# Where the second-level factors of w_out are summed: from row blocks in SBUF in the first group instead of from DRAM later, and two more products on two levels

## The chip, the cores and the metric

The kernel runs on one core of one Trainium2 chip. The time is that of one execution on the device, in microseconds (us), as the median of several runs. Before the change it is 671.21 us (three runs, 670.92 to 671.93).

## The reference

```python
# attention: batch 4, 8 heads, 768 positions, head size 64, blocks of 64 positions
intra = einsum('bhic,bhjc->bhij', qb, kb) * Dmask      # Dmask[i, j] = lam**(i-j) for i >= j
out   = einsum('bhij,bhjd->bhid', intra, vb) + einsum('bhid,bhde->bhie', qb * lam_pow, kv_state)
kv_state = lam_block * kv_state + einsum('bhsd,bhse->bhde', kb * rev_pow, vb)
# then, with x = out as (3072 tokens, 512)
h = x @ w_in                       # w_in (512, 2048), float64 on arrival
g = h - tanh(h)
result = g @ w_out                 # w_out (2048, 512), float64 on arrival
```

Everything is computed in fp32. Almost all of the time is in the two large matrix products.

## The kernel before

**Groups.** The 3072 tokens are taken in six groups (g = 0 to 5) of 512: 128 positions of each of the four batch entries. In a group, `up` computes the hidden values from x and w_in, the tanh step follows, and `down` computes the result from the hidden values and w_out. The attention of the next group is worked in between, in pieces (`att_transpose`, `att_scores`, `att_out`, `att_state`, `att_sums`), first for batch entries 0 and 1, then for 2 and 3.

**Products by Strassen and Winograd.** Both factors of a product are split in 2 x 2 blocks. Seven block products, numbered 1 to 7, take the place of eight; they need sums of blocks: S1 to S4 on one side, T1 to T4 on the other. `FACT` names the two factors of each of the seven: B11, B21, B22, T4, T1, T2 and T3 for products 1, 2, 3, 4, 5, 6 and 7 of `down`. A product of `down` on one level is sixteen matmuls (32 records in the profile, as an fp32 matmul shows as two) of 128x128 against 128x256. On two levels the same product is split once more in the same way: seven small products of four matmuls, 28 matmuls (56 records) of 128x128 against 128x128. `down` (lines 645 to 676) does the first and `down_twice` (696 to 732) the second; `twice(g, n)` says which product goes which way. Before the change the second group (g = 1) does products 5 and 6 on two levels, groups 2 to 4 do 3, 5, 6, 4 and 7, and the last group does 5, 6, 4 and 7.

**The first group.** Its `up` is plain. Its `down` goes over eight pairs of row blocks of w_out (`kt` = 0 to 7): rows kt x 128 and those 1024 further down, each split in two column halves, give b11, b12, b21 and b22. `round_block` makes fp32 of a loaded float64 block: ScalarE writes a copy into the pair's buffer and two halves of an addend, VectorE shifts the copy and adds. `sums_out(kt)` subtracts on VectorE to make T1, T2, T3 and T4 of that pair. `down_first` issues the matmuls of the pair, two for each of the seven products, which add up in seven PSUM banks (`acc`) over all eight pairs. `sums_late(kt)` makes two sums of the hidden values, the first of which overwrites what product 1 of this pair reads and is read by product 6. For a pair TensorE takes products 1, 2, then 5, 4, 7, 6, 3. `first_results` adds the seven banks up. Pairs have three buffers in turn: two of the pool `wst` and one made of `ws_3` and `ws_2`, which are free until the second group.

**Factors in DRAM.** `factors` holds the first-level factors, `fine` the seven second-level factors of each of five products (3, 5, 6, 4, 7). Of these seven, three are quarters of the first-level factor (small products 1, 2 and 3, one column half of an even or odd pair's rows), and `sums_out` stores them straight from the pair. The other four are sums of quarters. Before the change these are made in groups 1 and 2: `load_quarters` reads the four quarters of a first-level factor back from `factors`, and `factors_twice` makes four subtractions on VectorE and stores each result to `fine`, one at a time between other work, at the steps that `turns` gives: products 5 and 6 in the second group, 4, 7 and 3 in the third.

**Pieces.** The second factors of `down` come from DRAM as pieces of 256 KB through a ring of seven buffers (`wb`). `stream` lists them in the order of use, and `piece` hands out one and sends the loads of the next, on the queue of POOL (GpSimd).

**What sets the order.** Each engine works its instructions in order. A scheduler of the language orders them when the program is built, by its own estimate of when each is ready; `tc.keep_in_program_order` (also through `tied`) pins an instruction behind the one written just before it for the same engine. A tile with a tag takes one of the tag's buffers (`bufs`) and waits until the tile that had it is done. SyncE (SP) issues the loads of q, k and v, pinned in program order. From the third group on, k and v are loaded whole for two or three batch entries (`load_natural`, tags `k` and `v`, three and four buffers), and q and k also in blocks for transposes on VectorE (`load_blocks`, sixteen DMAs a tile, tag `blk`). In SP's order for a group stand k and v of entries 0 to 2 (third group) and then the eight tiles of blocks, with k and v of entry 3 after them.

Of the kernel before, what the change touches and what calls it, by code (L numbers as in the profile page):

```python
# [24 lines left out]
def kernel(  # L25
# [32 lines left out]
    nc = tc.nc  # L58
# [122 lines left out]
    NX = 7  # L181
# [40 lines left out]
    def weights(n):  # L222

        while ready["done"] < min(n, len(blocks)):
# [5 lines left out]
            w = w1[n_][:, m] if kind == "in" else pair[n_][0][:, 2 * m:2 * m + 2]  # L230
# [6 lines left out]
    def pair_tiles(kt):  # L237

        if kt % 3 == 2:
            return tuple(ws[u].rearrange("p x k c -> p (x k) c")[:, 0:4] for u in (3, 2))  # L240
        wt = wst.tile([128, 8, 256], F32, name="wt", tag="w")
        return wt[:, 0:4], wt[:, 4:8]
# [8 lines left out]
    def sums_out(kt):  # L251
        bt, tt = pair[kt]
        b11, b12, b21, b22 = (bt[:, x] for x in range(4))
        t1, t2, t4, t3 = (tt[:, x] for x in range(4))
        nc.vector.tensor_tensor(t1, b12, b11, op=AL.subtract)
# [12 lines left out]

    def round_block(w, raw64, first):
# [13 lines left out]
        tied(first, nc.vector.tensor_scalar(out=wb, in0=wb, scalar1=3, scalar2=None, op0=AL.logical_shift_left))  # L283
        nc.vector.tensor_tensor(wi, wi, add, op=AL.add)  # L284
# [264 lines left out]
    def twice(g, n):  # L549
        return n in TWICE and not (g == NG - 1 and n == 3) and not (g == 1 and n in (4, 7, 3))  # L550
# [27 lines left out]
    MADE = (5, 6, 4, 7, 3)  # L578
    quarters = {}

    def quarter_source(t, i, j):
        return factors[XAT[FACT[MADE[t]][1]]].rearrange("p (u m) c -> p u m c", m=2)[:, :, i, ts(j, 128)]

    def load_quarters(t):

        for i in range(2):
            for j in range(2):
                if t > 1:
                    quarters[t, i, j] = piece(2, ("quarter", t), 2 * i + j).rearrange("p m (v c) -> p (m v) c", v=2)
                    continue  # L590
                if t == 0:
                    x = late["pool"].tile([128, NU, 128], F32, name="wq", tag="wb", bufs=RING)
                else:
                    x = opool.tile([128, NU, 128], F32, name="oq", tag="o")
                nc.gpsimd.dma_start(out=x, in_=quarter_source(t, i, j))
                quarters[t, i, j] = x

    def factors_twice(t):

        b11, b12, b21, b22 = (quarters.pop((t, i, j)) for i in range(2) for j in range(2))  # L600
        t1, t2, t4 = (late["pool"].tile([128, NU, 128], F32, name=f"wt{x}", tag="sums", bufs=4) for x in (1, 2, 4))
        for x, dst, a, b in ((5, t1, b12, b11), (6, t2, b22, t1), (7, b12, b22, b12), (4, t4, b21, t2)):
            tc.keep_in_program_order(nc.vector.tensor_tensor(dst, a, b, op=AL.subtract))
            nc.gpsimd.dma_start(out=fine[TWICE.index(MADE[t]), SUB.index(x)], in_=dst)
            yield

    def piece(g, n, x):

        i = stream.index((g, n, x))
        while sent["n"] < min(i + RING, len(stream)):  # L610
            g_, n_, x_ = stream[sent["n"]]
            t = late["pool"].tile([128, 2, 256], F32, name="wb", tag="wb", bufs=RING)
            if isinstance(n_, tuple) and n_[0] == "quarter":
                nc.gpsimd.dma_start(out=t.rearrange("p m (v c) -> p (m v) c", v=2),
                                    in_=quarter_source(n_[1], *divmod(x_, 2)))
# [160 lines left out]
    FIRST = {1: (11, 0, 0), 2: (21, 0, 2), 3: (21, 0, 3), 4: (22, 1, 2), 5: ("S1", 1, 0), 6: (11, 1, 1), 7: (12, 1, 3)}  # L776
# [18 lines left out]
    def sums_late(kt):  # L795
        u, m = divmod(kt, 2)
        g11, g21, s1 = (hidden(0, c)[:, u, m] for c in (11, 21, "S1"))
        nc.vector.tensor_tensor(g11, s1, g11, op=AL.subtract)
        nc.vector.tensor_tensor(g21, g21, g11, op=AL.subtract)
# [76 lines left out]
    for kt in range(KH):  # L876
# [15 lines left out]
    turns = {1: (0, ((0, 7), (1, 14))), 2: (7 * NU, ((2, 1), (3, 5), (4, 9)))}  # L892
    made, making = [], {}
    load_quarters(0)
    load_quarters(1)
    up(1, 0, 1)
    for g in range(1, NG):
        last = g == NG - 1
        p0, p1 = attention(g + 1) if not last else ([], [])
        for u in range(NU):  # L900
            for n in (2, 6, 5, 7, 1, 4, 3) if g < GI else (1, 7, 3) if u == 0 else (6, 5, 1, 7, 3) if u + 1 < NU else (
# [9 lines left out]
                if g in turns:  # L911
                    made.append(n)
                    step = len(made) - turns[g][0]
                    for t, first in turns[g][1]:
                        if step == first:
                            if t > 1:
                                load_quarters(t)
                            making[t] = factors_twice(t)
# [71 lines left out]
```

## Time and profile before

| | before |
|---|---|
| median of the runs | 671.21 us |
| the profiled execution: time, span | 669.39 us, 667.6 us |
| TensorE (PE) busy | 655.6 us, 98% |
| VectorE (DVE) busy | 466.4 us, 70% |
| ScalarE (ACT) busy | 213.7 us, 32% |
| GpSimd (POOL) busy | 210.8 us, 32% |
| DMA | 128.82 MB, mean 193 GB/s |
| granted clock of TensorE | 1.0 |

The stretches of the span that matter here (us from its start): the pairs of the first group's `down`, 98.6 to 147.1; the second group's `up`, 147.1 to 204; its `down`, 204 to 262; the third group's `up` after that, to about 308. In a profile line the first number of a timeline row is the start, the second how long the row lasts from its first instruction's start to its last one's end; "x32" counts merged instructions, and a bracket tells how long the engine was idle before and what ended that. "L446" is a line of the kernel. In rows of waits the numbers are us in total, times, and the longest. A matmul's end is modelled, so lengths of products are read from start to start. "PEq", "SPq" and "POOLq" are the engines' queues.

### The profile page before, as it was taken

How to read it: one execution, taken by the hardware profiler on the slowest of the kernel's cores; microseconds unless marked ns; L12 is line 12 of the kernel's file. 1: busy time of each engine (PE TensorE's matmuls, PEld its weight loads, DVE VectorE, ACT ScalarE, POOL GpSimd, SP SyncE). 2: the span in 40 equal slices, each digit the busy share in tenths (PEclk: the TensorE clock that was granted, in tenths of full speed). 3: DMA queues.
4: the chain of work that ended last, by engine and by line, in shares of the span. 5: the costliest groups of instructions: out<-in, count | busy, mean ns of one | idle time of the engine just before them, and what ended most of it. 6: DMA issues, size and time to landing. Idle time of an engine off the chain costs nothing.

```text
span 667.6 us, 13061 instructions
## 1 busy us (share of the span) xinstructions
PE 655.6 (98%) x4920; PEld 594.1 (89%) x4920; DVE 466.4 (70%) x839; ACT 213.7 (32%) x402; POOL 210.8 (32%) x365
## 2 busy tenths in 40 slices
PE   7899999999999999999999999999999999999998
PEld 6688888888888989888999988999988899988897
DVE  4467896746988762599885379987368877357753
ACT  4787935503321112341112343112233112234110
POOL 0001445734522433254436101344300245400251
PEclk9999999999999999999999999999999999999999
DMA  9999988958855977568889533698730677610495
GB/s 209 223 201 261 286 306 234 342 160 233 229 133 137 235 188 205 150 198 259 239 260 280 142 76 75 170 274 255 215 70 17 158 237 219 219 37 0 120 295 170
DMA packets 163038, 128.82 MB, mean 193 GB/s; under 512 B 134176, under 2 KB 135328, under 8 KB 162976
## 3 DMA queue, kind: packets, MB, share of 16 engines
q0 software_dynamic: 29296, 96.49, 45.0%
q1 hardware_dynamic: 133536, 31.50, 24.0%
q8 instruction: 39, 0.64, 0.4%
q14 instruction: 23, 0.19, 0.1%
q10 hardware_dynamic: 144, 0.00, 0.0%
HBM read 103.55 MB, written 24.38 MB: 192 GB/s over the span
## 4 chain that ended last, share of the span: by engine, by line
PE 79%; issue 9%; DMA 5%; POOL 2%; SPq 2%; ACT 1%; DVE 1%; DVEq 0%; POOLq 0%; ACTq 0%
PE y L446 12%; PE y L708 10%; PE acc L792 7%; PE zw L708 7%; PE h L763 7%; PE z L446 7%; PE w L655 4%; PE y L655 4%; PE y L530 4%; PE plain L655 3%; PE sp L340 3%; PE op L394 3%; PE z L530 2%; DMA wb<-fine 2%; PE op L388 1%
## 5 line engine op out<-in xcount | busy, mean ns | idle before, releaser
L620 POOL DMA_DIRECT2D wb<-fine x147 | 79.4, 541 | 113.7 <-PE y L708 50.6
L623 POOL DMA_DIRECT2D wb<-factors x56 | 30.4, 543 | 155.9 <-PE y L655 99.7
L454 ACT ACTIVATE th<-g 128x512 f32<-128x512 f32 x76 | 47.7, 632 | 99.1 <-DVE g L459 33.2
L446 PE MATMUL y<-xt,w 128*128 128x256 f32 x320 | 74.0, 380 | 0.0
L446 PEld LDWEIGHTS y<-xt,w 128*128 128x128 f32 x320 | 59.9, 190 | 8.5 <-ACT g L534 0.9
L711 ACT ACTIVATE q<-y 128x128 f32<-128x128 f32 x84 | 23.3, 278 | 130.8 <-PE y L708 130.0
L455 DVE TENSOR_TENSOR g<-g,th 128x512 f32<-128x512 f32 x76 | 51.9, 688 | 16.8 <-ACT th L454 16.7
L763 PE MATMUL h<-xt,w 128*128 128x256 f32 x256 | 58.0, 383 | 2.3 <-DVE w L284 2.3
L763 PEld LDWEIGHTS h<-xt,w 128*128 128x128 f32 x256 | 47.7, 190 | 10.2 <-DVE w L284 2.6
L708 PE MATMUL y<-wb,g 128*128 128x128 f32 x384 | 51.1, 278 | 0.0
L708 PEld LDWEIGHTS y<-wb,g 128*128 128x128 f32 x384 | 46.4, 192 | 1.1 <-issue 0.3
L446 PE MATMUL z<-tt,ws 128*128 128x256 f32 x160 | 38.0, 380 | 0.0
L446 PE MATMUL z<-xt,ws 128*128 128x256 f32 x160 | 37.9, 380 | 0.0
L446 PE MATMUL y<-tt,ws 128*128 128x256 f32 x160 | 37.8, 379 | 0.0
L655 PE MATMUL y<-wb,g 128*128 128x256 f32 x160 | 35.6, 379 | 0.7 <-DVE g L465 0.7
L655 PE MATMUL w<-wb,g 128*128 128x256 f32 x160 | 35.8, 382 | 0.0
L344 DVE TENSOR_TENSOR ss<-sp,mask 128x512 f32<-128x512 f32 x48 | 31.1, 684 | 6.3 <-PE sp L340 6.3
L205 POOL DMA_DIRECT2D raw<-in_moe_w_out_dram x16 | 8.8, 549 | 84.7 <-ACT r L281 66.2
L655 PEld LDWEIGHTS y<-wb,g 128*128 128x128 f32 x160 | 30.3, 190 | 5.1 <-PE y L446 1.0
L446 PEld LDWEIGHTS z<-xt,ws 128*128 128x128 f32 x160 | 30.3, 190 | 4.3 <-ACT g L462 0.2
L655 PEld LDWEIGHTS w<-wb,g 128*128 128x128 f32 x160 | 30.1, 190 | 4.4
L708 PE MATMUL zw<-wb,g 128*128 128x128 f32 x256 | 33.8, 275 | 0.0
(198 smaller groups left out, 1349.6 us busy)
## 6 DMA issues: line engine op xcount, KB each, us to landing
wb<-fine POOLq DMA_DIRECT2D x147, 256.0 KB, 4.0
wb<-factors POOLq DMA_DIRECT2D x68, 256.0 KB, 4.2
raw<-in_moe_w_out_dram POOLq DMA_DIRECT2D x16, 512.0 KB, 5.8
v_nat<-in_v_dram SPq DMA_DIRECT2D x24, 256.0 KB, 5.2
fine<-wt POOLq DMA_DIRECT2D x24, 256.0 KB, 4.7
wb<-fine_in POOLq DMA_DIRECT2D x24, 256.0 KB, 4.2
k_nat<-in_k_dram SPq DMA_DIRECT2D x20, 256.0 KB, 4.9
raw<-in_moe_w_in_dram SPq DMA_DIRECT2D x8, 512.0 KB, 6.5
```

Source lines behind the costliest of these rows:

```text
L344: tied(g == 0, nc.vector.tensor_tensor(ss[:, j], sp[j], mask[:, j], op=AL.mult))
L446: nc.tensor.matmul(out=t[:, m, :], lhsT=wt[:, kt, ts(m, 128)], rhs=x[:, kt, :], start=first and m == 0 and kt == 0, stop=kt == 1, skip_gro ...
L454: nc.scalar.activation(th, src, AF.Tanh)
L455: nc.vector.tensor_tensor(dst(c), src, th, op=AL.subtract)
L530: nc.tensor.matmul(out=dst[:, ts(u, 128)], lhsT=a, rhs=b, start=x in (1, 2, 5) and u == 0, stop=True, skip_group_check=True)
L620: nc.gpsimd.dma_start(out=t.rearrange("p m c -> p (m c)"), in_=fine[TWICE.index(n_), SUB.index(x_)].rearrange("p u c -> p (u c)"))
L623: nc.gpsimd.dma_start(out=t, in_=factors[XAT[FACT[n_][1]]][:, 2 * x_:2 * x_ + 2, :])
L655: nc.tensor.matmul(out=t[:, m, :], lhsT=a[:, u, kt, ts(m, 128)], rhs=wb[:, kt, :], start=first and u == 0 and m == 0 and kt == 0, stop=u = ...
L708: nc.tensor.matmul(out=dst, lhsT=a[:, u, :], rhs=wb[:, ts(u, 128)], start=x in (1, 2) and u == 0, stop=u == NU - 1, skip_group_check=True)
L711: nc.scalar.activation(keep, dst, AF.Copy)
L763: tied(u == 0, nc.tensor.matmul(out=hm[c][:, m, :], lhsT=w1[u][:, i, a, ts(m, 128)], rhs=xt[0, t][:, i, :], start=m == 0 and i == 0, stop= ...
L792: nc.tensor.matmul(out=acc[n][:, r, :], lhsT=a[:, ts(r, 128)], rhs=b, start=kt == 0 and r == 0, stop=kt == KH - 1, skip_group_check=True)
```

## The change

The second-level sums of the four T factors (products 4, 5, 6 and 7) are made in the first group by a new function, `sums_fine(u)`, from two neighbouring pairs in SBUF: sixteen subtractions of 128x512 on VectorE, four for each u, with a store to `fine` after each. They are written into tiles of the tag `v`. `sums_fine` is called after the pairs 0, 2 and 4 and after `first_results`. With that, `factors` keeps three factors instead of seven, and `factors_twice` is left with product 3, in the third group. The pair's buffer is cut anew: b11 and b12 in one part, b21, b22 and the four T in the other, so that `sums_out` stores its rows of `fine` with one DMA where it took two. From `sums_out(1)` on, all that VectorE does for the pairs is pinned in program order (`sums_out`, `sums_late`, `sums_fine`, the rounding of the last ten blocks), and `sums_in(1)` moves from pair 2 to pair 5. Products 4 and 7 of the second group go on two levels.

```diff
-    NX = 7
+    NX = 3
     factors = dram.tile([NX, 128, KH, 256], F32, name="factors")
...
     def pair_tiles(kt):
         if kt % 3 == 2:
-            return tuple(ws[u].rearrange("p x k c -> p (x k) c")[:, 0:4] for u in (3, 2))
+            x, y = (ws[u].rearrange("p x k c -> p (x k) c") for u in (3, 2))
+            return x[:, 0:2], y[:, 0:6]
         wt = wst.tile([128, 8, 256], F32, name="wt", tag="w")
-        return wt[:, 0:4], wt[:, 4:8]
+        return wt[:, 0:2], wt[:, 2:8]
...
     def sums_out(kt):
-        bt, tt = pair[kt]
-        b11, b12, b21, b22 = (bt[:, x] for x in range(4))
-        t1, t2, t4, t3 = (tt[:, x] for x in range(4))
-        nc.vector.tensor_tensor(t1, b12, b11, op=AL.subtract)
-        nc.vector.tensor_tensor(t2, b22, t1, op=AL.subtract)
-        nc.vector.tensor_tensor(t3, b22, b12, op=AL.subtract)
-        nc.vector.tensor_tensor(t4, b21, t2, op=AL.subtract)
+        x, y = pair[kt]
+        b11, b12, b21, b22, t1, t2, t4, t3 = (t[:, i] for t, n in ((x, 2), (y, 6)) for i in range(n))
+        for dst, a, b in ((t1, b12, b11), (t2, b22, t1), (t3, b22, b12), (t4, b21, t2)):
+            tied(kt > 0, nc.vector.tensor_tensor(dst, a, b, op=AL.subtract))
         f = factors[:].rearrange("x p k c -> p x k c")
-        nc.gpsimd.dma_start(out=f[:, 0:1, kt, :], in_=bt[:, 0:1, :])
-        nc.gpsimd.dma_start(out=f[:, 1:3, kt, :], in_=bt[:, 2:4, :])
-        nc.gpsimd.dma_start(out=f[:, 3:NX, kt, :], in_=tt[:, 0:4, :])
-        for x, j in ((1, 0),) if kt % 2 == 0 else ((2, 0), (3, 1)):
-            dst = fine[:, SUB.index(x), :, kt // 2, :].rearrange("n p c -> p n c")
-            nc.gpsimd.dma_start(out=dst[:, 0:1], in_=bt[:, 3:4, ts(j, 128)])
-            nc.gpsimd.dma_start(out=dst[:, 1:5], in_=tt[:, 0:4, ts(j, 128)])
+        nc.gpsimd.dma_start(out=f[:, 0:1, kt, :], in_=x[:, 0:1, :])
+        nc.gpsimd.dma_start(out=f[:, 1:NX, kt, :], in_=y[:, 0:2, :])
+        for n, j in ((1, 0),) if kt % 2 == 0 else ((2, 0), (3, 1)):
+            nc.gpsimd.dma_start(out=fine[:, SUB.index(n), :, kt // 2, :].rearrange("n p c -> p n c"),
+                                in_=y[:, 1:6, ts(j, 128)])
+
+    def sums_fine(u):
+        (b11, b12), (b21, b22) = (tuple(pair[2 * u + i][1][:, 2:6, ts(j, 128)] for j in range(2)) for i in range(2))
+        t1, t2, t3, t4 = (io.tile([128, 4, 128], F32, name="fs", tag="v", bufs=4) for _ in range(4))
+        for x, dst, a, b in ((5, t1, b12, b11), (6, t2, b22, t1), (7, t3, b22, b12), (4, t4, b21, t2)):
+            tc.keep_in_program_order(nc.vector.tensor_tensor(dst, a, b, op=AL.subtract))
+            nc.gpsimd.dma_start(out=fine[1:5, SUB.index(x), :, u, :].rearrange("n p c -> p n c"), in_=dst)
...
     def round_block(w, raw64, first):
...
-        tied(first, nc.vector.tensor_scalar(out=wb, in0=wb, scalar1=3, ..., op0=AL.logical_shift_left))
-        nc.vector.tensor_tensor(wi, wi, add, op=AL.add)
+        late_block = ready["done"] >= NU * KI + 6
+        tied(first or late_block, nc.vector.tensor_scalar(out=wb, in0=wb, scalar1=3, ..., op0=AL.logical_shift_left))
+        tied(late_block, nc.vector.tensor_tensor(wi, wi, add, op=AL.add))
...
     def twice(g, n):
-        return n in TWICE and not (g == NG - 1 and n == 3) and not (g == 1 and n in (4, 7, 3))
+        return n in TWICE and not (n == 3 and g in (1, NG - 1))
...
     def pieces_of(g):
         if g == 2:
-            yield from ((g, ("quarter", t), x) for t in (2, 3, 4) for x in range(4))
+            yield from ((g, "quarter", x) for x in range(4))
...
-    MADE = (5, 6, 4, 7, 3)
-    def load_quarters(t):
...
-    def factors_twice(t):
-        b11, b12, b21, b22 = (quarters.pop((t, i, j)) for i in range(2) for j in range(2))
+    def factors_twice(g, n):
+        b11, b12, b21, b22 = (piece(g, "quarter", x).rearrange("p m (v c) -> p (m v) c", v=2) for x in range(4))
...
     def sums_late(kt):
-        nc.vector.tensor_tensor(g11, s1, g11, op=AL.subtract)
-        nc.vector.tensor_tensor(g21, g21, g11, op=AL.subtract)
+        tc.keep_in_program_order(nc.vector.tensor_tensor(g11, s1, g11, op=AL.subtract))
+        tc.keep_in_program_order(nc.vector.tensor_tensor(g21, g21, g11, op=AL.subtract))
...
         down_first(kt, (5, 4, 7, 6, 3) if kt + 1 < KH else (5, 6, 7, 4, 3))
+        if kt in (0, 2, 4):
+            sums_fine(kt // 2)
         if kt + 3 < KH:
             weights(ready["done"] + 2)
-        if kt == 2:
+        if kt == 5:
             sums_in(1)
     first_results()
+    sums_fine(3)
...
-    turns = {1: (0, ((0, 7), (1, 14))), 2: (7 * NU, ((2, 1), (3, 5), (4, 9)))}
-    load_quarters(0)
-    load_quarters(1)
     up(1, 0, 1)
...
-                if g in turns:
-                    made.append(n)
...
+                if g == 2 and u == 1 and n in (6, 5, 1, 7):
+                    if n == 6:
+                        making = factors_twice(g, 3)
+                    next(making)
```

More of the change, by code (lines that the diff above doesn't have):

```diff
@@ L229, in weights @@
                 pair[n_] = pair_tiles(n_)
-            w = w1[n_][:, m] if kind == "in" else pair[n_][0][:, 2 * m:2 * m + 2]
+            w = w1[n_][:, m] if kind == "in" else pair[n_][m][:, 0:2]
             if at_ in wraw:
@@ L281, in round_block @@
         tied(first, nc.scalar.activation(halves[:, :, 1], hif, AF.Copy, scale=2.0 ** -60))
-        tied(first, nc.vector.tensor_scalar(out=wb, in0=wb, scalar1=3, scalar2=None, op0=AL.logical_shift_left))
-        nc.vector.tensor_tensor(wi, wi, add, op=AL.add)
+        late_block = ready["done"] >= NU * KI + 6
+        tied(first or late_block, nc.vector.tensor_scalar(out=wb, in0=wb, scalar1=3, scalar2=None,
+                                                          op0=AL.logical_shift_left))
+        tied(late_block, nc.vector.tensor_tensor(wi, wi, add, op=AL.add))
     def bank(name, tag, bufs):
@@ L576 @@
     sent = {"n": 0}
-    MADE = (5, 6, 4, 7, 3)
-    quarters = {}
-    def quarter_source(t, i, j):
-        return factors[XAT[FACT[MADE[t]][1]]].rearrange("p (u m) c -> p u m c", m=2)[:, :, i, ts(j, 128)]
-    def load_quarters(t):
[L586 to L596, printed above, removed]
-    def factors_twice(t):
-        b11, b12, b21, b22 = (quarters.pop((t, i, j)) for i in range(2) for j in range(2))
+    def factors_twice(g, n):
+        b11, b12, b21, b22 = (piece(g, "quarter", x).rearrange("p m (v c) -> p (m v) c", v=2) for x in range(4))
         t1, t2, t4 = (late["pool"].tile([128, NU, 128], F32, name=f"wt{x}", tag="sums", bufs=4) for x in (1, 2, 4))
@@ L603, in factors_twice @@
             tc.keep_in_program_order(nc.vector.tensor_tensor(dst, a, b, op=AL.subtract))
-            nc.gpsimd.dma_start(out=fine[TWICE.index(MADE[t]), SUB.index(x)], in_=dst)
+            nc.gpsimd.dma_start(out=fine[TWICE.index(n), SUB.index(x)], in_=dst)
             yield
@@ L612, in piece @@
             t = late["pool"].tile([128, 2, 256], F32, name="wb", tag="wb", bufs=RING)
-            if isinstance(n_, tuple) and n_[0] == "quarter":
-                nc.gpsimd.dma_start(out=t.rearrange("p m (v c) -> p (m v) c", v=2),
-                                    in_=quarter_source(n_[1], *divmod(x_, 2)))
+            if n_ == "quarter":
+                i, j = divmod(x_, 2)
+                nc.gpsimd.dma_start(out=t.rearrange("p m (v c) -> p (m v) c", v=2), in_=factors[XAT["B22"]].rearrange(
+                    "p (u m) c -> p u m c", m=2)[:, :, i, ts(j, 128)])
             elif isinstance(n_, tuple):
@@ L775 @@
     ACC = {1: ("ya", 1), 2: ("w", 1), 5: ("z", 1), 6: ("yb", 1), 7: ("att", 4), 4: ("att", 4), 3: ("att", 4)}
-    FIRST = {1: (11, 0, 0), 2: (21, 0, 2), 3: (21, 0, 3), 4: (22, 1, 2), 5: ("S1", 1, 0), 6: (11, 1, 1), 7: (12, 1, 3)}
+    FIRST = {1: (11, 0, 0), 2: (21, 1, 0), 3: (21, 1, 1), 4: (22, 1, 4), 5: ("S1", 1, 2), 6: (11, 1, 3), 7: (12, 1, 5)}
     def sums_first(u):
@@ L889 @@
     late["pool"] = ctx.enter_context(tc.tile_pool(name="late", bufs=1))
-    turns = {1: (0, ((0, 7), (1, 14))), 2: (7 * NU, ((2, 1), (3, 5), (4, 9)))}
-    made, making = [], {}
-    load_quarters(0)
-    load_quarters(1)
     up(1, 0, 1)
@@ L910 @@
                     sums_in(u + 2)
-                if g in turns:
-                    made.append(n)
[L913 to L918, printed above, removed]
-                        if first <= step < first + 4:
-                            next(making[t])
+                if g == 2 and u == 1 and n in (6, 5, 1, 7):
+                    if n == 6:
+                        making = factors_twice(g, 3)
+                    next(making)
             if g == GI - 1:
```

## The prediction

> **What bounds the kernel now.** I read the page first, then the table of what TensorE waited for, then the timelines of TensorE, VectorE and SyncE around the places that the change touches.
>
> ```profile
> PE 655.6 (98%) x4920; PEld 594.1 (89%) x4920; DVE 466.4 (70%) x839; ACT 213.7 (32%) x402; POOL 210.8 (32%) x365
> ```
> TensorE is busy for 98% of the span and the clock row shows 9 in every slice, so time can be won in two ways only: less TensorE work, or one of its few gaps closed. After the first 30 us the waits list holds few gaps, and one of them lies in code that the change removes:
>
> ```profile
> PE h L763 <- DVE w L284: 2.3, 3, 0.9
> PE y L708 <- DMA wb<-fine: 1.0, 2, 0.8
> PE y L655 <- DVE g L465: 0.7, 1, 0.7
> ```
> The last row is at 298.2 us, where VectorE was late because four subtractions of line 603 (294.31 to 297.45 us) stood among its other work. Whatever the change adds off TensorE costs nothing until it makes TensorE wait, and costs its full length then. A product on one level, then one on two levels, by their starts:
>
> ```profile
> 215.28 7.17 PE L655 MATMUL plain<-wb,g 128*128 128x256 f32 x32
> 222.29 1.05 PE L708 MATMUL y<-wb,gS 128*128 128x128 f32 x8
> ...
> 228.64 2.06 PE L340 MATMUL sp<-qt,kt 64*128 64x128 f32 x32
> ```
> In the first group, for one pair of row blocks of w_out, VectorE and ScalarE do this (TensorE's 224 records from 98.60 to 147.14 us make 6.07 us a pair, so the second pair starts at 104.67):
>
> ```profile
> 104.88 1.24 ACT L279 ACTIVATE wt<-raw 128x512 f32<-128x512 f32 x2 [6.51 <-PE acc L792]
> 105.58 0.43 DVE L283 TENSOR_SCALAR wt<-wt 128x512 uint32<-128x512 uint32 x1 [3.49 <-ACT wt L279]
> 105.93 0.42 DVE L798 TENSOR_TENSOR g<-gS,g 128x256 f32<-128x256 f32 x1
> 106.26 0.68 DVE L284 CUSTOM_DVE_ANT_0 wt<-wt,r 128x1024 uint16<-128x1024 uint16 x1
> ...
> 108.14 0.42 DVE L255 TENSOR_TENSOR wt<-wt 128x256 f32<-128x256 f32 x1
> ```
> ScalarE copies a later pair only when TensorE has left the buffer; VectorE takes line 798 (sums_late) early, between the rounding steps. This interleaving is what the pins forbid. On SyncE:
>
> ```profile
> 100.19 0.93 SPq L131 DMA_DIRECT2D v_nat<-in_v_dram  x1
> 132.46 9.45 SPq L143 DMA_DIRECT2D q_blk<-in_q_dram  x16
> 141.95 7.89 SPq L143 DMA_DIRECT2D k_blk<-in_k_dram  x16
> ```
> The group 2 loads of v are issued by 101 us, and the blocks for its transposes from 132.46 on.
>
> **Two more products on two levels.** Products 4 and 7 of the second group each go from 7.01 us (215.28 to 222.29) to 6.35 us (222.29 to 228.64): -0.66 each, -1.3 us, all on TensorE. They bring six more piece loads, three VectorE sums before each, one inside and two after, and ScalarE copies of 0.28 us. The same product in the third group (323.44 to 329.85) ran without a gap over its piece loads. I charge 0.2 us, for a busy VectorE at 237.5 to 246 us, where TensorE already loses 0.4 us at 239.8; between 0 and one sum's 0.6.
>
> **The quarters leave groups 1 and 2.** Sixteen quarter loads, sixteen of twenty subtractions (0.605 us from start to start) and as many stores go. The eight of the second group, at 165 to 182 us, were hidden: TensorE does not wait there. In the third group four of twelve remain, earlier, so the gap at 298.2 us should close: -0.7. At worst it stays.
>
> **sums_out and DRAM.** A pair stores 2 factors and not 7, and its fine rows; with sums_fine an even and an odd pair come to 11 issues of POOL where there were 12, and the same bytes: 2752 KB (2 x 896 + 960 before, 2 x 384 + 960 + 1024 after). The sums of sums_fine leave in rows of 512 bytes where the T factors left in rows of 1 KB, and the DMA engines are busy for 92 to 100% of 111 to 135 us. At its two ends it is relieved: of most of the k and v loads of group 2 (landing until 105 us) and of the first blocks (from 132.46). In POOL's queue the four stores of a sums_fine (0.75 us each) stand ahead of the next two loads of w_out. The last such load was issued at 119.39, landed at 126.75 and its block was rounded at 131.71: with ScalarE's two halves (1.4 us) 3.5 us are to spare, against 3.0. Behind sums_fine(3) stand the first piece loads; four stores take the place of eight quarter loads there (147.7 to 155.8), so they go sooner. Cost 0; if this cover goes, a late load costs what it is late, 1 to 2 us.
>
> **The fixed order on VectorE.** From sums_out(1) on everything is one chain. After TensorE leaves a pair: ScalarE's copy and the first shift at +0.91 (105.58 less 104.67); rounding of two blocks 0.35 + 0.60 + 0.34 + 0.61 = 1.90; sums_out, four at 0.33 to 0.45, 1.45; then the first of sums_late, 0.42. That ends at +4.68. TensorE wants it for product 6, the sixth of seven, at 20/28 of 6.07 = +4.34; with 0.1 for the signal (ScalarE answered TensorE in 0.21) it is 0.4 us late, for each of the five pairs 1 to 5: 2.0 us. sums_fine adds four of 128x512, 4 x 0.605 + 0.1 = 2.5 us, in pairs 0, 2 and 4: its end, at +0.91 + 1.90 + 1.45 + 0.75 + 2.5 = +7.5, is 0.1 after the next pair's first shift would run (6.07 + 0.4 + 0.91 = 7.4). For pairs 0 and 4 the next copy takes over the very buffer that its third sum reads, and comes 0.4 later. Together 0.8, so 2.8. What waits is TensorE's product 6, and behind it product 3 and the next pair. But TensorE's order is not pinned, and the language's scheduler can put the next pair's first product (0.87 us) ahead where it expects the wait. Floor 0 (reordered so each time), ceiling 4.0 (the four sums at their full durations of 0.42, 0.23 us more a pair); I take +2.6, close to the sum, since TensorE kept program order in before's timeline. sums_in(1) moves from pair 2 to pair 5, where 2.5 us of VectorE are free before pairs 6 and 7, which round nothing: 0.
>
> [...]
>
> **The loads of v wait.** The sums of sums_fine live in the ring of four buffers named v, whose tiles are handed out in the order in which the code first writes them. So the v loads of group 2 come after sums_fine(3), behind first_results. Its first sum starts at 148.83 us (line 814 at 148.22, plus 0.61); POOL is free of the output stores at 150.6; a store landed 2.5 to 3.8 us after its issue in this stretch, so 154.0; the third is 1.5 later, and with the loads of k and v SyncE begins its blocks at 156.5 instead of 132.46. In its queue stand eight tiles of sixteen issues. Tiles took 7.9 to 9.25 us (the latter 74 us for all eight), 8.5 in the middle; plus 1.7 to landing the last is there at 226.2, between 221.4 and 232.2. Before it landed at 207.7 and was transposed at 221.83. After, that transpose stands behind product 4's end, as in the third group, where it came 8.94 us after that product's start (323.44 to 332.38): 215.28 + 8.94 = 224.2. So it is 2.0 late, and behind it in VectorE's order are a multiply and the line 713 sum that TensorE needs inside product 5, with 0.6 to spare there: 1.4 us, from 0 to 7.4. I take +1.0, as the scheduler may put the sum first.
>
> [...]
>
> **The sum** against the profiled execution's own 669.39 us (its span of 667.6 and 1.8 around it): -1.3 - 0.7 + 0.2 + 2.6 + 1.0 = +1.8. That execution was 1.8 below the median of 671.21 (670.92 to 671.93); on the median it gives 673.0.
>
> **The rivals.** *Faster.* The scheduler moves each next first product ahead of product 6, and the first group loses 0.4 rather than 2.6; the blocks go at 7.9 us a tile and arrive in time. Then -1.3 - 0.7 + 0.2 + 0.4 = -1.4: 669.8. Place: TensorE's order in 104 to 136 us. It decides once the first group's loss and the loads' together stay under 1.8. For it: VectorE has 18 of 48 us free in the first group before. Against: the chain is late by less than a matmul, which a scheduler's estimate may not see.
>
> *SyncE decides.* At 8.9 us a tile (the next group's seven took 61.2, 8.7 each, and the worst tile 12) the last block lands at 229.4, 5.2 late, and TensorE loses 4.6: +5.4, 676.6. For it: SyncE issues in order, and one late v stops all 128 block loads. Against: before had 14 us to spare.
>
> *Nothing comes of it.* The products are shorter, but the gap at 298.2 us stays behind another of VectorE's sums and the chain costs just what is won: within 0.5 us of before.
>
> **How the numbers follow.** About 0.2% (1.3 us) is what a measurement of this kernel can tell from no change. Forecast 0.42, from +0.4 to +3.0: 0.29 slower, 0.13 same. Faster rival 0.30, from -2.0 to -0.4: 0.21 faster, 0.09 same. SyncE 0.22, all slower. Nothing 0.06, half same and half slower. So 0.21 faster, 0.25 same, 0.54 slower. The range goes from 669.2 (-2.0: every added wait hidden) to 677.0 (+5.8: the SyncE rival and a little more); under 0.15 is left outside. The forecast's own is 671.6 to 674.2.
>
> **What would show it.** Two more products of 6.3 us at lines of down_twice in the second group; no gap at 298; waits of TensorE's acc for line 798's sum, some 0.4 us each, in 104 to 137 us; block loads from about 156 us; the last transpose of k near 226 and TensorE waiting after it. I am wrong if acc shows no gaps with the products in their old order (the chain is then shorter than its rows), if the blocks start before 150, or if a gap of over 2 us opens where I named none, the second group's first products at 148 to 165 us above all, where sums_fine(3) stands ahead of VectorE's other work.

## The result, and the profile after

The changed kernel takes 688.27 us (median of 6 runs, 685.63 to 689.25), the kernel before beside it on the same chip 671.38 (6 runs, 669.65 to 671.93). The ratio is 1.0245, 95% interval 1.0221 to 1.0269: slower by 2.45%. The forecast was 673.0 with a range to 677.0. It had the sign right and the size wrong by 15 us. The profiled execution after took 689.25 us with a span of 687.5; the one before had 669.39 and 667.6. So the two traces differ by 19.9 us, 3 more than the medians.

The page of the changed kernel, busy time of the engines and the clock row:

```profile
PE 662.6 (96%) x4968; PEld 599.1 (87%) x4968; DVE 477.2 (69%) x851; ACT 214.7 (31%) x409; POOL 194.1 (28%) x335
...
PEclk9999999999999979999999999999999999999999
```

TensorE has 24 more matmuls (48 records), and one slice of the clock row (240 to 258 us) is not a 9 any more. The share of busy time fell by 2 points only, because matmuls at half clock count as busy (1.00 us of the stretch 250 to 251 us, at a clock of 0.50).

What TensorE waited for in the changed kernel, from 60 to 270 us (line, releaser, us in total, times, longest):

```profile
PE zw L695 <- DVE gS L700: 7.7, 1, 7.7
PE acc L779 <- DVE g L785: 2.6, 4, 0.8
PE kv L368 <- issue: 2.6, 1, 2.6
PE h L750 <- DVE w L290: 1.9, 1, 1.9
```

The gap of the kernel before at 298 us is gone, the four waits of acc are the ones that the prediction named (line 785 is the first sum of sums_late, 798 before), and the wait of 7.7 us is new. SyncE in the changed kernel:

```profile
160.25 0.37 SPq L131 DMA_DIRECT2D v_nat<-in_v_dram  x1
161.14 0.96 SPq L131 DMA_DIRECT2D k_nat<-in_k_dram  x1
162.28 4.26 SPq L131 DMA_DIRECT2D v_nat<-in_v_dram  x1
166.65 3.34 SPq L131 DMA_DIRECT2D k_nat<-in_k_dram  x1
170.16 2.78 SPq L131 DMA_DIRECT2D v_nat<-in_v_dram  x1
173.03 8.80 SPq L143 DMA_DIRECT2D q_blk<-in_q_dram  x16
...
230.82 8.62 SPq L143 DMA_DIRECT2D k_blk<-in_k_dram  x16
```

The v loads do wait for the stores of sums_fine(3), as the prediction said, but the blocks start at 173.03, not at 156.5, and the last is issued until 239.44. VectorE and then TensorE around it:

```profile
209.36 0.71 DVE L325 STREAM_TRANSPOSE kt<-k_blk 128x512 f32<-128x512 f32 x1 [8.20 <-DMA q_blk<-in_q_dram]
...
235.80 0.70 DVE L325 STREAM_TRANSPOSE qt<-q_blk 128x512 f32<-128x512 f32 x1
243.50 0.71 DVE L325 STREAM_TRANSPOSE kt<-k_blk 128x512 f32<-128x512 f32 x1 [7.00 <-DMA k_nat<-in_k_dram]
244.13 0.65 DVE L336 TENSOR_TENSOR qd<-qt,fwd 128x512 f32<-128x512 f32 x1
244.70 0.68 DVE L700 TENSOR_TENSOR gS<-gS,s 128x512 f32<-128x512 f32 x1
```

```profile
236.65 1.06 PE L695 MATMUL y<-wb,gS 128*128 128x128 f32 x8
245.44 2.07 PE L695 MATMUL zw<-wb,gS 128*128 128x128 f32 x8 [7.73 <-DVE gS L700]
247.31 1.91 PE L695 MATMUL y<-wb,gS 128*128 128x128 f32 x8
249.15 2.97 PE L346 MATMUL sp<-qt,kt 64*128 64x128 f32 x32
```

VectorE stands 7 us at the last k transpose, with the sum that product 5 needs two places behind it. After the wait the eight records of a step take 1.87 us from start to start instead of 0.89: the clock has halved. The stretches of that time (PEclk is the third number from the end):

```profile
245.40:248.00 2.60, 2.56 (x12) 2.56 (x13) 1.66 (x4) 0.00 (x0) 0.19 (x1) 0.50 0.22 34
...
250.00:251.00 1.00, 1.00 (x12) 1.00 (x12) 0.00 (x0) 0.00 (x0) 0.06 (x1) 0.50 0.75 186
251.00:253.00 2.00, 2.00 (x28) 1.88 (x25) 1.74 (x3) 0.00 (x0) 0.00 (x0) 0.97 0.58 143
```

An account of the 20.8 us by which the trace is behind at the end of product 7 (269.17 against 248.39 us), by the starts of the same steps in both traces:

| stretch | before | after | lost |
|---|---|---|---|
| up to the first matmul of acc | 98.53 | 100.72 | 2.2 |
| the stage of acc, to the first matmul of group 1 | 48.45 long | 52.76 long | 4.3 |
| to the kv of the next group's attention | 214.25 | 224.02 | 3.3 |
| that kv, at half clock | 1.03 | 1.91 | 0.9 |
| product 4 | 7.01 | 7.15 | 0.1 |
| product 5 | 6.35 | 16.07 | 9.7 |
| the scores behind it | 1.98 | 2.90 | 0.9 |
| product 7 | 7.01 | 6.36 | -0.65 |

The first row is not the change's: TensorE waited 2.3 us for a rounded weight block at 66.6 us (1.3 before, in code that both share), and its clock was at half from 70.2 to 73.6. In the twelve traces of this case the first matmul of acc starts anywhere from 97.3 to 100.7 us, in no order that follows the edits.

### The profile page after: what moved, and what is told of

It reads as the page before. It is cut to its first block, busy times and chain, and to the rows that moved or that the text cites. A ratio compares the mean times of both kernels' runs of the same rounds, so it can differ in the third digit from the quotient of the medians.

```text
span 687.5 us, 13141 instructions
## 1 busy us (share of the span) xinstructions
PE 662.6 (96%) x4968; PEld 599.1 (87%) x4968; DVE 477.2 (69%) x851; ACT 214.7 (31%) x409; POOL 194.1 (28%) x335
## 4 chain that ended last, share of the span: by engine, by line
PE 63%; DMA 10%; SPq 8%; DVE 7%; issue 5%; POOL 3%; ACT 3%; DVEq 0%; POOLq 0%; ACTq 0%
PE y L452 12%; PE y L695 10%; PE z L452 8%; PE zw L695 7%; SPq L143 5%; PE y L536 4%; PE y L642 4%; PE w L642 3%; PE h L750 3%; DMA raw<-in_moe_w_in_dram 3%; PE sp L346 3%; DMA raw<-in_moe_w_out_dram 3%; PE z L536 2%; PE op L400 2%; DMA wb<-fine 2%
## 5 line engine op out<-in xcount | busy, mean ns | idle before, releaser
L607 POOL DMA_DIRECT2D wb<-fine x161 | 86.9, 540 | 140.9 <-PE y L695 56.4
L698 ACT ACTIVATE q<-y 128x128 f32<-128x128 f32 x92 | 25.6, 278 | 158.4 <-PE y L695 157.0
L610 POOL DMA_DIRECT2D wb<-factors x48 | 26.0, 543 | 166.0 <-PE y L642 105.1
L750 PE MATMUL h<-xt,w 128*128 128x256 f32 x256 | 60.0, 391 | 2.8 <-DVE w L290 2.8
L695 PE MATMUL y<-wb,g 128*128 128x128 f32 x432 | 58.2, 280 | 0.0
L695 PEld LDWEIGHTS y<-wb,g 128*128 128x128 f32 x432 | 52.9, 194 | 1.3 <-issue 0.3
L695 PE MATMUL zw<-wb,g 128*128 128x128 f32 x288 | 38.1, 275 | 0.0
L779 PE MATMUL acc<-wt,g 128*128 128x256 f32 x144 | 33.9, 383 | 1.6 <-DVE g L785 1.5
L695 PEld LDWEIGHTS zw<-wb,g 128*128 128x128 f32 x288 | 35.0, 192 | 0.1
L642 PEld LDWEIGHTS y<-wb,g 128*128 128x128 f32 x160 | 30.4, 190 | 4.1
```

Source lines behind the costliest of these rows:

```text
L607: nc.gpsimd.dma_start(out=t.rearrange("p m c -> p (m c)"), in_=fine[TWICE.index(n_), SUB.index(x_)].rearrange("p u c -> p (u c)"))
L610: nc.gpsimd.dma_start(out=t, in_=factors[XAT[FACT[n_][1]]][:, 2 * x_:2 * x_ + 2, :])
L642: nc.tensor.matmul(out=t[:, m, :], lhsT=a[:, u, kt, ts(m, 128)], rhs=wb[:, kt, :], start=first and u == 0 and m == 0 and kt == 0, stop=u = ...
L695: nc.tensor.matmul(out=dst, lhsT=a[:, u, :], rhs=wb[:, ts(u, 128)], start=x in (1, 2) and u == 0, stop=u == NU - 1, skip_group_check=True)
L750: tied(u == 0, nc.tensor.matmul(out=hm[c][:, m, :], lhsT=w1[u][:, i, a, ts(m, 128)], rhs=xt[0, t][:, i, :], start=m == 0 and i == 0, stop= ...
L779: nc.tensor.matmul(out=acc[n][:, r, :], lhsT=a[:, ts(r, 128)], rhs=b, start=kt == 0 and r == 0, stop=kt == KH - 1, skip_group_check=True)
```

## The experiments

The time beside each is the median, the ratio is to runs of the kernel before on the same chip. "Stage of acc" is always from its first matmul to the first of group 1, 48.45 us before and 52.76 after.

**The block loads first.**

```
-            first = (0, 1, 2) if g == GB else ()
+            first = ()
```

> The changed kernel with one line of load() different: SyncE issues the block loads of group 2 ahead of that group's natural loads, so no block load stands behind a v load that waits for the sums of sums_fine. All is computed. Theory *late blocks* (the stall of 8.0 us at 237, the wait of 2.85 us at 221 and the slow matmuls after each come from the blocks that start at 173 us in the place of 132): the blocks start at 138 to 141 us, the last k transpose no longer waits, and 13 to 15.6 us come back: 673 to 676 us. Rival *VectorE is too full* (the three new sums ahead of product 4 and the first group's chain make TensorE wait, wherever the loads are): TensorE still waits over 5 us between 215 and 250, and the time stays above 682.

673.28 us, ratio 1.0061 (1.0042 to 1.0079). The blocks start at 136.46 us:

```profile
136.46 9.65 SPq L143 DMA_DIRECT2D q_blk<-in_q_dram  x16
...
205.60 9.80 SPq L143 DMA_DIRECT2D k_blk<-in_k_dram  x16
```

The waits at 221 and 237 us are gone, the clock is 1.000, and 1.84 points of the 2.45 came back (12.3 us of 669.5, a little under the 13 to 15.6 expected). The stage of acc is 52.75 us as in the changed kernel. So the late blocks are the larger cause, and the rest of VectorE's work was not too much for it.

**Late loads in the kernel before.** Behind first_results():

```
+        for x in range(4):
+            t = io.tile([128, 32], F32, name="hold", tag="v", bufs=4)
+            tc.keep_in_program_order(nc.vector.tensor_copy(t, hold_from["q5"][:, 0:32]))
+            nc.gpsimd.dma_start(out=scratch[x], in_=t)
```

> The kernel before, with four small tiles put in the ring of v behind first_results (VectorE copies 32 columns of its last result into each, POOL stores each to a scratch of DRAM): the loads of v of group 2 then wait for these stores, and nothing else of the change is in it. All is computed, and a scratch is written besides. Theory *late blocks*: the blocks start at 160 to 168 us, the last lands at 228 to 236 where VectorE's queue holds it at 222, TensorE stalls 5 to 10 us in product 5 or just before it and its clock drops after that: 678 to 688 us. Rival *VectorE is too full*: without the extra sums there is room on VectorE, and the time is within 2 us of the 671.3 before.

686.99 us, ratio 1.0264 (1.0245 to 1.0284). Nothing of the change is in it but the place of the v loads, and it costs as much as the whole change. Blocks from 160.81 us, and TensorE waits twice (from 60 to 350 us):

```profile
PE zw L708 <- DVE gS L713: 6.1, 1, 6.1
PE z L446 <- DVE g L477: 5.6, 2, 5.1
```

Behind each of the two the clock stays at 0.50, for 3.9 and 3.5 us. The delay of one ring is enough on its own.

**The order free, the blocks first.** On top of the first edit:

```
-            tied(kt > 0, nc.vector.tensor_tensor(dst, a, b, op=AL.subtract))
+            nc.vector.tensor_tensor(dst, a, b, op=AL.subtract)
...
-        late_block = ready["done"] >= NU * KI + 6
+        late_block = False
...
-        tc.keep_in_program_order(nc.vector.tensor_tensor(g11, s1, g11, op=AL.subtract))
-        tc.keep_in_program_order(nc.vector.tensor_tensor(g21, g21, g11, op=AL.subtract))
+        nc.vector.tensor_tensor(g11, s1, g11, op=AL.subtract)
+        nc.vector.tensor_tensor(g21, g21, g11, op=AL.subtract)
```

> The kernel of blocks_first, with the fixed VectorE order of the first group taken off: the four sums of sums_out, the late rounding steps and the two sums of sums_late are free again as they are before the change; sums_fine and sums_in keep theirs. All is computed. Theory *the order costs* (the 4.3 us that the stage of acc grew by come from the fixed chain that ends in line 785's sum): the stage falls to 49 to 50 us and the time is 2.5 to 4 us under blocks_first. Rival *the work costs* (the four new sums of each sums_fine fill VectorE and the order is beside the point): within 1 us of blocks_first, the stage still 52 us or more.

667.76 us (11 runs, 666.62 to 668.67), ratio 0.9971 (0.9955 to 0.9987): 0.3% under the kernel before. The stage of acc is 48.45 us again, with all four sums_fine in it. The two orders for pair 1, first the changed kernel's (pair from 107.10 us), then the free one (from 104.75):

```profile
108.48 0.43 DVE L288 TENSOR_SCALAR wt<-wt 128x512 uint32<-128x512 uint32 x1 [0.20 <-ACT wt L283]
108.94 0.69 DVE L290 CUSTOM_DVE_ANT_0 wt<-wt,r 128x1024 uint16<-128x1024 uint16 x1
109.55 0.65 DVE L288 TENSOR_SCALAR wt<-wt 128x512 uint32<-128x512 uint32 x1
110.23 0.69 DVE L290 CUSTOM_DVE_ANT_0 wt<-wt,r 128x1024 uint16<-128x1024 uint16 x1
110.84 0.88 DVE L256 TENSOR_TENSOR ws<-ws 128x256 f32<-128x256 f32 x2
111.64 0.42 DVE L256 TENSOR_TENSOR ws<-ws,ws 128x256 f32<-128x256 f32 x1
111.97 0.42 DVE L256 TENSOR_TENSOR ws<-ws 128x256 f32<-128x256 f32 x1
112.31 0.42 DVE L785 TENSOR_TENSOR g<-gS,g 128x256 f32<-128x256 f32 x1
```

```profile
105.66 0.65 DVE L288 TENSOR_SCALAR wt<-wt 128x512 uint32<-128x512 uint32 x1 [0.96 <-ACT wt L283]
106.22 0.41 DVE L785 TENSOR_TENSOR g<-gS,g 128x256 f32<-128x256 f32 x1
106.55 0.68 DVE L290 CUSTOM_DVE_ANT_0 wt<-wt,r 128x1024 uint16<-128x1024 uint16 x1
107.16 0.41 DVE L288 TENSOR_SCALAR wt<-wt 128x512 uint32<-128x512 uint32 x1
107.49 0.41 DVE L786 TENSOR_TENSOR g<-g,g 128x256 f32<-128x256 f32 x1
107.83 0.68 DVE L290 CUSTOM_DVE_ANT_0 wt<-wt,r 128x1024 uint16<-128x1024 uint16 x1
```

The sum that TensorE waits for starts at +5.21 us in the fixed order and at +1.47 in the free one. VectorE does the same work in both. The median fell by 5.5 us (0.90 points) where the stage accounts for 4.3; the two intervals leave room for the rest.

**The order free alone.** The same edit to the changed kernel, the v loads left where they are.

> The changed kernel with the fixed VectorE order of the first group taken off as in blocks_free, but the loads of v still behind sums_fine's ring and the blocks behind them. All is computed. Theory *two separate costs*: the stage of acc falls to 49 us, the blocks start 4 us sooner with it but as late against TensorE as they were, and the stall near 230 us stays: 683 to 685. Rival *one cause* (the blocks are late because the first group is): the stall goes as well, and the time is under 676.

683.00 us, ratio 1.0186 (1.0159 to 1.0212), 0.59 points under the changed kernel. The stage is 48.45 us, the blocks start at 166.99, 6 us sooner, and the stall stays:

```profile
PE zw L695 <- DVE gS L700: 8.6, 1, 8.6
```

Two separate costs: taking either away leaves the other.

**The order fixed, in the kernel before.** There, without any sums_fine:

```
+        tied(kt > 0, nc.vector.tensor_tensor(t1, b12, b11, op=AL.subtract))   (and t2, t3, t4)
+        late_block = ready["done"] >= NU * KI + 6   (and the two rounding steps tied to it)
+        tc.keep_in_program_order(nc.vector.tensor_tensor(g11, s1, g11, op=AL.subtract))   (and g21)
-        if kt == 2:
+        if kt == 5:
```

> The kernel before, with the change's fixed VectorE order alone: sums_out from pair 1 on, the rounding of the late blocks and sums_late keep program order, and sums_in(1) stands at pair 5. No sums_fine, no product moved. All is computed. Theory *the order costs*: the chain copy, rounding, sums_out, first sum of sums_late is late for product 6 in each pair without any help from sums_fine. My prediction's rows made this 0.4 us a pair, 2.0 in all; from the stalls of the changed kernel (0.44 to 1.15 us at each of five pairs) I now expect 2 to 4 us, so 671.5 to 673.5 where the kernel before has 669.5. Rival *the order costs only with sums_fine in it*: the stage of acc stays within 0.5 us of 48.5, and the time within 1 us of before.

673.55 us, ratio 1.0047 (1.0026 to 1.0067). The stage is 51.88 us: the order alone costs 3.4 of the 4.3 us, and with sums_fine inside it the total is 0.9 more. By the starts of every 28th record the pairs 0 to 6 take 6.38, 6.37, 6.37, 7.22, 6.38, 6.86 and 6.26 us, where before they take 6.15 and then 6.04 each. So three of the pairs 1 to 5 lose 0.33 us, close to the 0.4 of the rows, and pairs 3 and 5 lose 1.18 and 0.82. What is different there, ScalarE and VectorE at pair 3:

```profile
119.28 0.78 ACT L280 ACTIVATE r<-raw 128x512 int16<-128x512 uint32 x1 [2.44 <-DMA raw<-in_moe_w_out_dram]
```

```profile
121.22 0.43 DVE L284 TENSOR_SCALAR ws<-ws 128x512 uint32<-128x512 uint32 x1 [2.20 <-ACT ws L279]
...
123.76 0.42 DVE L800 TENSOR_TENSOR g<-gS,g 128x256 f32<-128x256 f32 x1
```

A raw block of w_out landed late, ScalarE waited for it, VectorE for ScalarE, and in a fixed order the sum for TensorE stands behind. At pair 5 it is the same (ScalarE waits 2.81 us for a raw block until 132.42). In the kernel before the raw block comes late too (ScalarE waits 2.55 us for it until 121.19), but line 798 goes ahead of its rounding, at 119.01.

**Another fixed order.** On top of blocks_first:

```
-        if kt + 1 < KH:
-            sums_out(kt + 1)
         sums_late(kt)
+        if kt + 1 < KH:
+            sums_out(kt + 1)
```

> The kernel of blocks_first, with sums_late(kt) put ahead of sums_out(kt + 1), all still in a fixed order. All is computed. Theory *the order costs*: after the rounding (0.91 + 1.90 us from a pair's start) the first sum of sums_late ends near +3.3, a microsecond before product 6 wants it at +4.34, sums_out has till the next pair's products, and the stage of acc falls to 49 to 50 us: 2.5 to 4 us under blocks_first. Rival *the work costs*: the wait moves to the next pair's first products, which wait for sums_out instead; within 1 us of blocks_first.

672.25 us, ratio 1.0053 (1.0035 to 1.0071), within the noise of blocks_first; the stage 52.05 us. By the starts of every 28th record only two pairs still lose, 1.3 us at pair 3 and 2.3 at pair 5; this is pair 5:

```profile
131.90 0.68 DVE L270 TENSOR_TENSOR fs<-ws,fs 128x512 f32<-128x512 f32 x1
134.13 0.49 DVE L288 TENSOR_SCALAR wt<-wt 128x512 uint32<-128x512 uint32 x1 [1.55 <-ACT wt L283]
...
136.33 0.42 DVE L785 TENSOR_TENSOR g<-gS,g 128x256 f32<-128x256 f32 x1
```

Here a raw block was late again: ScalarE had waited 1.82 us for it until 132.18, and the sum still has the whole rounding ahead of it. At pair 3 the record shows no wait for a raw block; there the rounding, and with it the sum, stands behind sums_fine(1), four sums from 116.45 to 119.07 us. My expectation was wrong: it took the sums of the rows and no wait. The rival is right in its outcome and wrong in its mechanism, for the next pair's first products do not wait for sums_out.

**Only sums_late free.** On top of blocks_first, the last four lines of the free edit.

> The kernel of blocks_first with only the two sums of sums_late free of the fixed order; sums_out and the late rounding keep it. All is computed. Theory *the sum behind the chain* (TensorE waits because sums_late may not go between the rounding steps, where VectorE waits for ScalarE): the stage of acc falls from 52.75 to 48.5 to 49.5 us and the time to that of blocks_free, 667 to 669. Rival *the rounding behind the sums* (with the rest fixed the rounding and sums_out come late as well, and the next pair waits for them): the stage stays above 50.5.

671.13 us, ratio 1.0016 (1.0001 to 1.0030). The stage is 50.48 us, half way. Pairs 0 to 4 now take 6.04 to 6.15 us each as before the change, and what is left is 1.7 us at pair 5 and 0.3 at pair 6, behind line 786, the second sum of sums_late (1.4 us of wait in the record). So neither theory holds whole: the sum in the chain is the larger part, and with the rest fixed a late block still reaches TensorE at the end.

**Product 5 and the transposes.** Products 4 and 5 of the second group take 14.5 us together in blocks_free (the tiles put the boundary at 222.03 us, so 6.68 and 7.83, and not 8.1 as the expectation has it). On top of it:

```
-        run(p1[0:1])
         sums_once(g, 21, 21, 11)
         sums_twice(g, 6)
+        if g != 1:
+            run(p1[0:1])
         every(down_twice(g, 5, "w"))
-        run(p1[1:2])
+        run(p1[0:2] if g == 1 else p1[1:2])
```

> The kernel of blocks_free, with the transposes and scores of the second half of the next group's attention set behind product 5 in place of ahead of it, in the second group alone. All is computed. In blocks_free product 5 of the second group takes 8.1 us from start to start (221.70 to 229.86) where before has 6.35: its a12 sum (line 700) stands behind four transposes and two multiplies on VectorE. Theory *VectorE at product 5*: the sum goes ahead, product 5 falls to 6.4 to 6.9 us, and 1 to 1.8 us come back: 666 to 667. Rival *the same wait later* (VectorE's work does not shrink, and product 6 or the scores wait in place of product 5): within 0.5 us of blocks_free.

669.20 us, ratio 0.9988 (0.9972 to 1.0003), not faster than blocks_free. With the sum ahead of the transposes product 5 still waits in the same place, and the record says for what, as it does in blocks_free:

```profile
223.10 1.13 PE L695 MATMUL zw<-wb,gS 128*128 128x128 f32 x8
224.94 1.13 PE L695 MATMUL y<-wb,s 128*128 128x128 f32 x8 [0.71 <-DMA wb<-fine]
```

These are lines of blocks_free. The piece of the fine factors is late, not VectorE. My theory fell; the next pair of runs holds the other.

**Fewer pieces.** On blocks_free, product 4 on one level (blocks_free_p7), or 4 and 7 (blocks_free_p0, with NX = 5):

```
-    NX = 3
+    NX = 4
+        nc.gpsimd.dma_start(out=f[:, 3:NX, kt, :], in_=y[:, 4:NX + 1, :])
-        return n in TWICE and not (n == 3 and g in (1, NG - 1))
+        return n in TWICE and not (n == 3 and g in (1, NG - 1)) and not (n == 4 and g == 1)
```

> The kernel of blocks_free, with product 4 of the second group on one level again as it is before the change; its factor T4 is stored to DRAM once more (eight stores of 128 KB by POOL). Product 7 of that group stays on two levels. All is computed. In blocks_free products 4 and 5 of the second group take 14.5 us together (215.35 to 229.86) where before has 13.4 (215.28 to 228.64). Theory *product 4 costs its neighbour more than it saves* (its three sums ahead, and one inside, push VectorE's transposes and product 5's sum back): product 4 goes back to 7.0, product 5 to 6.4 from 8.1, and the time is 0.7 to 1.5 us under blocks_free, near 666.5 where the kernel before has 669.5. Rival *product 5 is slow for another reason* (the blocks that come after the natural loads, or its pieces): product 5 stays at 8 us and the time rises 0.5 to 1 us.

> The kernel of blocks_free, with products 4 and 7 of the second group both on one level as they are before the change; T4 and T3 are stored to DRAM once more. What is left of the change: the fine T factors made in the first group, and no quarters in it and the second. All is computed. Theory *product 7 saves its 0.66 us and product 4 nothing*: 0.6 us over blocks_free_p7 and 0.1 to 0.9 under blocks_free. Rival *both save 0.66 us*: 1.3 us over blocks_free.

668.19 us, ratio 0.9975 (0.9957 to 0.9992), and 668.61, ratio 0.9992 (0.9977 to 1.0007). In the trace of blocks_free_p7 product 4 takes 7.01 us (215.87 to 222.88), product 5 6.34 (to 229.22), and the record has no wait of TensorE from 69 to 270 us. The stretch 220 to 225 us, in blocks_free and in blocks_free_p7 (the last two numbers are the share of the DMA engines and GB/s):

```profile
220.00:225.00 5.00, 4.21 (x34) 3.81 (x33) 4.83 (x10) 0.83 (x3) 2.43 (x6) 1.00 1.12 319
```

```profile
220.00:225.00 5.00, 5.00 (x35) 4.64 (x33) 3.82 (x7) 0.87 (x2) 2.04 (x4) 1.00 1.08 259
```

Seven pieces of 256 KB in 6.35 us are 289 GB/s by themselves, where four in 7.01 are 150. Product 5 goes at the pace of its pieces: in blocks_free they landed at 222.97, 224.81, 225.75 and 226.64 us, and its steps start 0.13 to 0.16 us behind each. A piece's load is issued when its buffer in the ring of seven comes free (for the pieces of fine, line 607, POOL waits for TensorE's y of line 695 76 times in blocks_free, 55.9 us in all), some 5 us ahead of its use at this pace, and it took up to 6.3 us to land, where blocks_free_p7 has 3.5 to 4.9. That the DMA engines are the limit in this place, with block and natural loads beside the pieces, is read from the bytes and not shown by a run; a ring with more buffers, which would send the pieces sooner, was not tried. As to time, blocks_free and blocks_free_p7 cannot be told apart (0.9971 and 0.9975), though the trace has 1.15 us between them up to there; the 0.6 us expected between p7 and p0 are inside the intervals too. The expectation named VectorE as the way in which product 4 costs its neighbour; the traces show the pieces.

## Why the prediction was wrong

**The loads of v: +1.0, and it was 12.3** (14.4 with the order free, from 1.0186 to 0.9971). This is the step that failed. Its mechanism was right link by link as far as it went (the ring, the order in which tiles are handed out, SyncE held up, 16 issues a tile, the last k transpose, and the sum behind it in VectorE's queue). Three sizes were wrong.

- The start of the blocks, 156.5 against 173.03. 6.5 us of it is that the first group ended that much later (sums_fine(3) starts at 155.32, not 148.83); 2.2 of them are the later start of acc, which is not the change's, and for the rest the prediction had its own +2.6 and did not add it here. The other 10 are the loads between the third store's landing (162.4) and the first block: I took 1.0 us for the two v and the k left, and SyncE was 4.26, 3.34 and 2.78 us in single issues, while POOL's seven piece loads were in flight (the DMA engines 0.99 and 1.12 busy in 164 to 173 us); what holds a single issue so long no run isolates. The tiles themselves took 8.3 us each, near the 8.5 of the sum.
- What a late block costs. The sum had one transpose 2.0 us late and one sum behind it. VectorE had already stood 8.2 us at an earlier block (201 to 209 us), and what it owed then, among it the decay of k (line 355, 223.23 us, where blocks_free has it from 212.17), made TensorE wait 2.6 us at kv: a gap of over 2 us where none was named, one of the prediction's own signs of being wrong.
- The clock. No step had it. The half clock after the waits at 221 and 237 us costs some 4 us: 0.9 at the kv, 0.5 in product 4 (7.15 against the 6.68 of blocks_free), 1.8 in product 5 (16.07 less the wait of 7.9 and 6.35) and 0.9 in the scores.

The ceiling of 7.4 us was therefore no ceiling: it held the tiles at their slowest and neither the start nor what follows a stall. The rival *SyncE decides* named the right engine and had the same start, so its +4.6 was short as well.

**The fixed order: +2.6, and it was 4.3 in the trace.** Right in kind: acc waits for line 785. The term of 2.0 for the order alone measured 3.4 (before_pinned), and sums_fine, put at 0.8, added 0.9 to that. In the pairs of before_pinned where every input was there the 0.4 of the rows measured 0.33. What the sum lacked there was a late raw block: I had put the loads of w_out at 0, with 3.0 us to spare, and 1 to 2 us if that cover goes. It went at pairs 3 and 5, and cost 1.3 us beyond the 0.33 of the others.

The changed kernel does not lose its time in the same way. Its three longest waits of acc (0.75 to 0.77 us) stand in pairs 1, 3 and 5, each behind a sums_fine, and only at pair 5 was a raw block late as well. Pair 1 loses 1.04 us, 0.71 more than in before_pinned. Of this 0.49 is the start of the rounding, which comes at +1.38 us from the pair's start instead of +0.89, since ScalarE's copy waits for the sums of sums_fine(0) to leave the buffer, as the prediction had it with 0.4:

```profile
107.76 1.28 ACT L283 ACTIVATE wt<-raw 128x512 f32<-128x512 f32 x2 [7.21 <-DVE fs L270]
```

The other 0.22 is the rounding itself, 2.36 us (108.48 to 110.84) against 2.14 in before_pinned (106.13 to 108.27): one of its shifts takes 0.65 us in place of 0.42, for which no run shows the reason. Both are over the 1.90 of the prediction: I had read its steps from a free order, where other work fills the time that each waits for the one before (in the fixed order a shift and the add behind it start 0.46 us apart, 108.48 and 108.94, where the prediction has 0.35). The ceiling of 4.0 was passed. TensorE's order did drift by one matmul a pair, as the rival *Faster* had it, and the waits stayed.

**Products 4 and 7: -1.3 and +0.2.** With the loads in place (blocks_free) product 7 takes 6.35 us and product 4 6.68, with a pause of 0.2 in it for VectorE's sum of line 700: -1.0, where -1.1 was forecast. But product 5 is 1.5 us longer for its pieces, which no term had. "Ran without a gap over its piece loads" was read from the third group and was the false step: in the second, with the loads in the order of blocks_first, the same pieces meet more loads. In the trace the two products so lose 0.5 us in sum; the times do not resolve it (0.9971 with both, 0.9975 with product 7 alone, 0.9992 with neither, all intervals overlapping). No run has both products without a stall and with the loads in the order of the kernel before.

**The gap at 298 us: -0.7.** No two starts lie more than 0.31 us apart from 262 to 330 us in the changed kernel, where the kernel before has 1.05 us at 297.2. Right. sums_in(1) at no cost, too: pair 6, behind it, has 0.05 us of wait in the line of its late sum.

**The rest of the net.** Without the two costs the change is worth 0.29% (0.13 to 0.45), 1.9 us, against the -1.4 of the rival *Faster*. That rival asked for both waits to vanish by the scheduler's hand; one line on the loads and the order left free do it. How much of the 1.9 us is the change's own is open, for the kernel before was not run with the blocks ahead of the natural loads.

## What to carry to other kernels

Before a new tile is put into an existing ring, write down what its release waits for and what stands behind the next load of that ring in its queue; here a ring of four buffers of 256 KB held up 128 transfers that had nothing to do with it, and a different order of issue removed 12.3 us. Cost a fixed order of instructions with every wait of its inputs, late loads above all, for it gives up what a free order does in those waits; in this kernel that was 3.4 us in 48. Where a product is cut into more and smaller factors, compare the bytes that it asks for in its own time with what the DMA engines have free in that place: here a product that asked for 289 GB/s where it had asked for 150 left the next one 1.5 us longer in the trace, more than the 1.0 us that the two products gained.

## What the runs showed of the hardware

Each of the four long waits of TensorE in these traces was followed by a stretch at half clock. After waits of 8.0 us (changed kernel), 8.9 (free_order), 6.4 and 5.5 (before_late), each from the last start ahead of it to the first one behind it, the granted clock stayed at 0.50 for another 3.5 to 5.7 us. In the changed kernel the records of a 128-column matmul stood 213 ns apart there (246 to 249 us) where they stand 112 apart, and those of a 256-column one at the half clock of 70.2 to 73.6 us 426 ns where they stand 216 apart. Of the shorter waits, those of 2.29 and 2.85 us in the changed kernel brought it on (with the first it began 1.3 us after the wait's end), and those of 2.39 (blocks_late1st), 2.32 (free_order) and 2.17 us (blocks_latefree) did not.

In these traces it goes by where the wait lies. Within a trace all falls and rises of the clock are a whole number of 3.41 us apart, up to the end of the work (1, 44, 1, 4 and 3 times between the six of the changed kernel). The changed kernel, cut into windows at these places (the first number behind the comma is TensorE's busy time):

```profile
66.78:70.19 3.41, 1.50 (x7) 1.22 (x7) 2.97 (x6) 3.41 (x7) 1.06 (x2) 1.00 1.08 300
70.19:73.61 3.42, 3.42 (x10) 2.73 (x9) 3.22 (x7) 3.42 (x7) 0.53 (x1) 0.50 0.97 302
...
244.27:247.69 3.42, 2.25 (x10) 2.25 (x11) 2.48 (x5) 0.00 (x0) 0.00 (x0) 0.50 0.26 40
247.69:251.10 3.41, 3.41 (x26) 3.19 (x26) 1.28 (x3) 0.28 (x1) 1.08 (x2) 0.50 0.60 126
```

In the traces the clock fell six times ahead of the end of the work, each time at the end of a window in which TensorE was busy for 1.50 us or less (1.50, 1.07 and 0.26 in the changed kernel, 1.23 and 0.52 in before_late, 0.15 in free_order). Two windows with 1.50 us, in free_order and blocks_latefree, passed without a fall, and so did all with more. It rose only at the end of a window with 3.19 us or more, and not after one with 2.25. So a wait of 2 to 3 us was hit or spared by its place, and behind a long one the half clock lasted for the rest of the window and a whole one.

The wait itself can be a third shorter than the window: that of 2.29 us (66.56 to 68.85 us) brought the clock down at 70.19. What it is worth in time: the stall of 8.0 us cost 2.7 us more behind it (1.8 in product 5 and 0.9 in the scores).
